# Attention and routed experts on one core: the sign turns of later groups and their adding transfers stand 4 to 11 half-steps later

## The chip, the cores and the metric

The kernel runs on one core of a Trainium2 chip. The metric is device time in microseconds (us) of one execution; the median of the runs is compared. Engine names in the rows are PE (TensorE matmul; PEld is its weight load), DVE (VectorE), ACT (ScalarE), POOL (GpSimd) and SP (SyncE, which here only issues transfers). A "q" behind a name is the engine's sequencer.

## What is computed

Attention over 32 heads (batch 4, 8 heads, 768 positions, 64 dimensions) in which a query sees only the keys of its own bucket, followed by a layer of eight experts with 384 places each:

```python
q_bits = (np.einsum('bhsd,dk->bhsk', q, proj) > 0)      # 6 sign bits make a bucket, keys alike
mask = q_bucket[:, :, :, None] == k_bucket[:, :, None, :]
scores = np.where(mask, scale * np.matmul(q, k.transpose(0, 1, 3, 2)), -1000000000.0)
scores = scores - np.max(scores, axis=-1, keepdims=True)
attn = np.exp(scores); attn = attn / (np.sum(attn, axis=-1, keepdims=True) + 1e-09)
x = np.matmul(attn, v)                                  # then rows of 512 = 8 heads x 64
# each row goes to one expert, best logits first: out = relu(x @ w1[e]) @ w2[e]
```

## The kernel before

Queries, keys and values are float32, and every product is made of float16 pairs: a rounded value ("high") and what rounding left over ("low"). The 32 heads are eight groups of four (G = 0 to 7). Of group G the transposed queries and keys are loaded to `qp` and `kp`. ACT rounds them to `qh` and `kh` (`cast`, line 147). The low parts `ql` and `kl` are `qp - qh` and `kp - kh`. In groups 1 and 2 POOL subtracts them (line 149). From group 3 on it is done in two other steps: ACT writes `-qh` into `ql` (`turn`, line 151, once for each of two head pairs), and then a transfer, issued by POOL, adds the float32 queries from memory onto it as it writes (`adds`, line 153). The same goes for the keys.

SP then moves high and low parts to where the matmuls read them: `qa`, `ka` get the high parts and sign bits, `qb` and `kb` a high and a low part. These are the moves (`moves`, with `go` at line 198, sign bits at line 204, clearing at line 214, next loads at line 76). `qa`, `ka`, `qb` and `kb` exist twice, for even and odd groups. The buffers `qp`, `kp`, `qh`, `kh`, `ql` and `kl` exist once: `turn` of one group writes the `ql` that the moves `qb<-ql` of the group before still have to read.

The main loop runs over 192 steps: six blocks of 128 keys for each head. In a step PE makes the score matmuls of a later head for its maxima (`S_pass`, line 265, reduced by DVE at line 267), the transposed scores of this head in two halves (`ST`, lines 314 and 315, into one of three buffers `pst`), and the product of weights and values four steps behind (`AV`, lines 337 to 339). ACT takes the exponential of each half (line 316, `pt<-pst`), and POOL or DVE makes its low part (`lo`, lines 320 and 323). The norm and the output of two heads follow (`XS`, low part on DVE at line 365, transfers by SP at line 375).

Other work is written into the loop by a table of half-steps: two in a step, 48 in a group. Entries count from the start of the group before, so half-step +1 of group G falls after the first scores of group G-1. For groups 4 to 7 the moves stand at +1 (high parts, sign bits, next `qp`) and +9 (clearing, next `kp`, then `kb<-kl` and `qb<-ql`). The table `Z4` places the turns at -31, -19, -25 and -13 (queries and keys of the first pair of heads, then of the second) and the adds at -19 (queries) and -11 (keys). As a group has 48 half-steps, -31 is +17 of the group before: eight half-steps behind the moves that read the same `ql`.

```python
def turn(G,w,p):
    A.activation(TMP[G,'l'][w][:,p],TMP[G,'h'][w][:,p],AF.Copy,scale=-1.0)
def adds(G,w):
    G_.dma_start(TMP[G,'l'][w]...,(qT,kT)[w][G]...,accum_op=ALU.add)
# in the loop over groups G, n = 0..3: w = n%2 (queries, keys), head pair n//2
z=AP['Z3'] if G==3 else [48*(G-1)+x for x in AP['Z4']]
add(z[n],turn,G,n%2,n//2)
if n<2: add(z[4+n],adds,G,n)
```

Every engine runs its instructions in the order in which they are written, and waits at the first that isn't ready.

Of the kernel before, what the change touches and what calls it, by code (L numbers as in the profile page):

```python
# [39 lines left out]
 LT=[362, 4],  # L40
 MS=74,
 Z3=[77,85,88,91,93,97],
 Z4=[-31,-19,-25,-13,-19,-11],
 EA=[262, 32, 5],
 EG={2: 0, 3: 3},
 MO=['', 'AKs', 'BqL', 'lmk', 'c|ABqKLslmk', 'ABqKLs|cklm', 'ABqKLs|cklm'],
# [9 lines left out]
def attention(tc, nc, ctx, qT, kT, vv, proj, wg, x_dram, L, jp, identf, ident, B, late=None, after=None):  # L56
# [343 lines left out]
    def add(n,f,*a):  # L400
        if n>=2*(6*NH+LAG+6): raise ValueError('an operation has no step')
        at.setdefault(n,[]).append((f,a))
# [15 lines left out]
    for G in range(1,NG):  # L418
# [5 lines left out]
        for n in range(4):  # L424
            if G<3: add(p[8+n],sub,G,n%2,n//2)
            else:
                z=AP['Z3'] if G==3 else [48*(G-1)+x for x in AP['Z4']]
                add(z[n],turn,G,n%2,n//2)
# [618 lines left out]
```

## Time and profile before

| | us |
|---|---|
| median of 3 runs (lowest, highest) | 743.61 (742.87, 745.62) |
| the profiled execution | 746.34 |
| its span | 744.6 |
| PE busy | 663.9 (89%) |
| DVE busy | 532.0 (71%) |
| POOL busy | 503.5 (68%) |
| ACT busy | 391.7 (53%) |

The attention takes a little more than the first half of the span and the experts the rest. PE is the busiest engine, and in most of the 40 slices of the page it is busy 90% or more; the dips in its first half are what there is to look at. To read them, one takes first who waited for whom, then the rows of the waiting engines in order of time.

### The profile page before, as it was taken

The numbers are of one execution on the slowest core, as the hardware profiler recorded it, in microseconds if no ns is written. First come the engines' busy times: TensorE is split into PE (matmuls) and PEld (weight loads), VectorE is DVE, ScalarE is ACT, GpSimd is POOL, SyncE is SP. The second block draws the span as 40 slices with busy tenths as digits, with TensorE's granted clock in tenths as the row PEclk, the third lists the DMA queues.
The fourth block names the chain that finished last, engine by engine and source line by source line (L and its number), as shares of the span: only waits on it lengthen the run. The fifth ranks groups of instructions, "written<-read, shape, count | busy, mean of one in ns | idle before, by whom it ended". The sixth has DMA issues, their size and how long they took to land. (4 is left out here: it accounts for less than half of the span.)

```text
span 744.6 us, 19011 instructions
## 1 busy us (share of the span) xinstructions
PE 663.9 (89%) x7761; PEld 425.5 (57%) x7769; DVE 532.0 (71%) x1230; ACT 391.7 (53%) x801; POOL 503.5 (68%) x464
## 2 busy tenths in 40 slices
PE   8999999499599688699999769999999999999994
PEld 2666666367366456467777556555555555555552
DVE  6879889378388486488898784989878887843120
ACT  6876886466466545567556225343535353444430
POOL 7799987367477456477775054485877878787761
PEclk9999999799799899899999759999999999999998
DMA  8649768667576655676131243536271717072601
GB/s 213 194 108 199 180 177 165 129 104 166 121 140 176 122 95 122 130 135 137 38 47 45 65 135 137 174 124 223 89 270 42 270 42 279 34 283 70 256 28 43
DMA packets 64299, 102.54 MB, mean 138 GB/s; under 512 B 28960, under 2 KB 53588, under 8 KB 62164
## 3 DMA queue, kind: packets, MB, share of 16 engines
q1 hardware_dynamic: 55236, 51.10, 29.0%
q0 software_dynamic: 8224, 50.08, 22.4%
q8 instruction: 61, 1.00, 0.6%
q10 hardware_dynamic: 752, 0.15, 0.1%
q14 instruction: 26, 0.21, 0.1%
HBM read 67.39 MB, written 12.58 MB: 107 GB/s over the span
## 5 line engine op out<-in xcount | busy, mean ns | idle before, releaser
L320 POOL TENSOR_TENSOR lo<-pt 128x768 f16<-128x768 f32 x148 | 240.3, 1644 | 105.5 <-ACT pt L316 96.5
L267 DVE TENSOR_REDUCE m<-pss 128x1 f16<-128x770 f32 x192 | 181.4, 956 | 71.3 <-PE pss L265 70.3
L316 ACT ACTIVATE pt<-pst 128x384 f32<-128x384 f32 x384 | 172.5, 489 | 100.6 <-PE pst L315 94.0
L314 PE MATMUL pst<-qa,ka 128*128 128x384 f16 x384 | 128.3, 335 | 38.3 <-ACT pt L316 33.8
L337 PE MATMUL psv<-vh,pt 128*128 128x65 f16 x1152 | 128.1, 197 | 3.4 <-DVE X L355 3.4
L315 PE MATMUL pst<-qb,kb 128*128 128x384 f16 x384 | 128.5, 335 | 0.0
L339 PE MATMUL psv<-vh,lo 128*128 128x65 f16 x1152 | 127.6, 196 | 0.8 <-POOL lo L320 0.6
L338 PE MATMUL psv<-vl,pt 128*128 128x64 f16 x1152 | 127.9, 195 | 0.0
L337 PEld LDWEIGHTS <-pt 128*128 128x128 bf16 x1152 | 109.3, 100 | 20.8 <-DVE X L355 5.3
L338 PEld LDWEIGHTS <-pt 128*128 128x128 bf16 x1152 | 108.2, 100 | 12.0 <-issue 1.7
L339 PEld LDWEIGHTS <-lo 128*128 128x128 f16 x1152 | 108.1, 99 | 1.2 <-POOL lo L320 0.9
L864 ACT CAST wh<-wf 128x1024 f16<-128x1024 f32 x64 | 65.4, 1042 | 76.7 <-DMA wf<-in_w_dram,zwidx 55.8
L265 PE MATMUL pss<-ka,qa 128*128 128x385 f16 x384 | 97.7, 339 | 7.2 <-DVE m L267 6.4
L876 POOL TENSOR_TENSOR wl<-wf,wh 128x512 bf16<-128x512 f32 x74 | 84.1, 1151 | 0.2 <-issue 0.2
L315 PEld LDWEIGHTS <-kb 128*128 128x128 f16 x384 | 38.1, 99 | 59.7 <-issue 39.5
L899 PEld LDWEIGHTS <-wh 128*128 128x128 f16 x544 | 50.6, 99 | 31.2 <-issue 1.4
L855 POOL DMA_INDIRECT wf<-in_w_dram,zwidx x20 | 19.9, 994 | 57.2 <-DVE zmi L788 30.6
L899 PE MATMUL ph<-xx,wh 128*128 128x384 f16 (+1 forms) x304 | 57.2, 313 | 0.4 <-issue 0.3
L911 PEld LDWEIGHTS <-hh 128*128 128x128 f16 x384 | 35.5, 97 | 36.3
L314 PEld LDWEIGHTS <-ka 128*128 128x128 f16 x384 | 38.3, 100 | 28.8 <-DMA qa<-mr 4.0
L899 PE MATMUL po<-xx,wh 128*128 128x384 f16 x240 | 48.1, 326 | 0.0
L986 POOL TENSOR_TENSOR wl<-wf,wh 128x512 bf16<-128x512 f32 x36 | 42.6, 1211 | 4.2 <-ACT wh L864 3.5
(292 smaller groups left out, 1215.8 us busy)
## 6 DMA issues: line engine op xcount, KB each, us to landing
vp<-in_vv_dram SPq DMA_DIRECT2D x8, 768.0 KB
x_dram<-XS SPq DMA_DIRECT2D x16, 384.0 KB
qp<-in_qT_dram SPq DMA_DIRECT2D x7, 768.0 KB
kp<-in_kT_dram SPq DMA_DIRECT2D x7, 768.0 KB
qa<-qh SPq DMA_DIRECT2D x14, 192.0 KB
ka<-kh SPq DMA_DIRECT2D x14, 192.0 KB
qb<-qh SPq DMA_DIRECT2D x14, 192.0 KB
kb<-kh SPq DMA_DIRECT2D x14, 192.0 KB
```

Source lines behind the costliest of these rows:

```text
L265: T.matmul(ps[:,hf,0:HK],QA[u][:,j,qc*128:qc*128+128],KA[u][:,j,hf*HK:hf*HK+HK],start=True,stop=True)
L267: V.tensor_reduce(M6[h][:,qc:qc+1],ps[:,:,0:HK],axis=AX.XY,op=ALU.max,negate=True)
L314: T.matmul(ps[:,0:384],KA[u][:,j,kr],QA[u][:,j,r],start=True,stop=False)
L315: T.matmul(ps[:,0:384],KB[u][:,j,kr],QB[u][:,j,r],start=False,stop=True)
L316: A.activation(PT[h,kc][0][:,r],ps[:,0:384],AF.Exp,scale=0.125)
L320: eng.tensor_tensor(l,p,p.bitcast(BF)[:,1::2],op=ALU.subtract)
L337: T.matmul(av[:,c,:],ph[:,r],VH[u][:,j,kc,:],start=(kc==0 and c==0),stop=False,skip_group_check=True)
L338: T.matmul(av[:,c,0:64],ph[:,r],VL[u][:,j,kc,:],start=False,stop=False,skip_group_check=True)
L339: T.matmul(av[:,c,:],l[:,r],VH[u][:,j,kc,:],start=False,stop=False,skip_group_check=True)
L864: s.nc.scalar.copy(h[:,r],f[:,r])
L876: for _ in range(n): s.nc.gpsimd.tensor_tensor(*s.pend.pop(0)[1],op=ALU.subtract)
L899: T.matmul(p[:,r],a[:,o:o+128],b[:,d,r],start=n==0 and not c,stop=n==11 and c in (None,2),skip_group_check=c is not None)
```

## The change

The table `Z4` gets other numbers. It serves groups 4 to 7; group 3 has a table of its own and groups 1 and 2 have no turns.

```diff
- Z4=[-31,-19,-25,-13,-19,-11],
+ Z4=[-20,-12,-18,-9,-15,-6],
```

So the query turns move from -31 and -25 to -20 and -18, the key turns from -19 and -13 to -12 and -9, and the adds from -19 to -15 (queries) and from -11 to -6 (keys). No instruction is added or taken away. PE's and SP's instructions stand in the same order in both, and so do DVE's.

ACT, between the value casts of group 4 and the keys of group 5 (`vh` is a value cast, `qh` and `kh` are the roundings, `ql` the turn, `pt` an exponential), before:

```order
L216 CAST vh_215<-vp 128x6x64
L151 ACTIVATE ql<-qh 128x768
L316 ACTIVATE pt<-pst 128x384
L216 CAST vh_215<-vp 128x6x64
L316 ACTIVATE pt<-pst 128x384
L147 CAST qh<-qp 128x384
L316 ACTIVATE pt<-pst 128x384 x2
L147 CAST qh<-qp 128x384
L316 ACTIVATE pt<-pst 128x384 x2
L151 ACTIVATE ql<-qh 128x768
```

The same engine in the changed kernel, from nine exponentials behind the place where the first turn stood (`mr` is a row of maxima, `shi` a sum of values):

```order
L282 ACTIVATE mr<-pst,mb_198,ms_199 24x128
L316 ACTIVATE pt<-pst 128x384
L231 CAST shi<-pst 32x256
L147 CAST kh<-kp 128x384
L285 DMA qa_171<-mr 4x6x128
L316 ACTIVATE pt<-pst 128x384
L151 ACTIVATE ql<-qh 128x768
L316 ACTIVATE pt<-pst 128x384 x2
L151 ACTIVATE ql<-qh 128x768
L316 ACTIVATE pt<-pst 128x384
L147 CAST kh<-kp 128x384
```

The first turn of the queries stood between two value casts; now eleven exponentials, both remaining roundings of the queries and two of the keys stand ahead of it. The key turns follow on the same engine:

```order
L316 ACTIVATE pt<-pst 128x384 x2
L363 CAST XS<-X 128x6x128
L316 ACTIVATE pt<-pst 128x384
L151 ACTIVATE kl<-kh 128x768
L316 ACTIVATE pt<-pst 128x384 x2
L282 ACTIVATE mr<-pst,mb_198,ms_199 24x128
L316 ACTIVATE pt<-pst 128x384
L151 ACTIVATE kl<-kh 128x768
```

The first key turn passed both later roundings of the keys, both turns passed the rounding of `XS`, and the second, which passed the row of maxima too, stands three exponentials behind the first instead of six.

On POOL, at the adds of group 5 (`lo` is a low part; `wt`, `wtb`, `tiny` are small constants), the changed kernel against the one before:

```order
-L153 DMA ql<-in_qT_dram 128x1536
 L574 TENSOR_SCALAR wt<-wt_88 128x8
+L153 DMA ql<-in_qT_dram 128x1536
 L575 TENSOR_SCALAR wtb<-wt_88 128x8
 L320 TENSOR_TENSOR lo<-pt 128x768 x2
-L153 DMA kl<-in_kT_dram 128x1536
 L551 MEMSET tiny 128x1
-L320 TENSOR_TENSOR lo<-pt 128x768 x8
+L320 TENSOR_TENSOR lo<-pt 128x768 x2
+L153 DMA kl<-in_kT_dram 128x1536
+L320 TENSOR_TENSOR lo<-pt 128x768 x6
```

The add of the queries passes one small constant and no low part, and the add of the keys passes two low parts.

## Rows read from the trace of the kernel before

**Rows 1.** Who waited for whom, whole run: us in total, times, longest.

```profile
PE pst L314 <- ACT pt L316: 33.8, 5, 9.9
ACT ql L151 <- DMA qb<-ql: 32.7, 4, 9.2
```

**Rows 2.** Timeline of ACT, the four waiting turns: start, length, instruction, [idle before <-releaser].

```profile
139.38 0.84 ACT L151 ACTIVATE ql<-qh 128x768 f16<-128x768 f16 x1 [9.20 <-DMA qb<-ql]
...
194.48 0.84 ACT L151 ACTIVATE ql<-qh 128x768 f16<-128x768 f16 x1 [8.91 <-DMA qb<-ql]
...
246.91 0.84 ACT L151 ACTIVATE ql<-qh 128x768 f16<-128x768 f16 x1 [7.86 <-DMA qb<-ql]
...
306.74 0.84 ACT L151 ACTIVATE ql<-qh 128x768 f16<-128x768 f16 x1 [6.75 <-DMA qb<-ql]
```

**Rows 3.** Timeline of SP, the end of the moves ahead of the second wait.

```profile
184.16 0.48 SPq L76 DMA_DIRECT2D kp<-in_kT_dram  x1
184.75 1.35 SPq L198 DMA_DIRECT2D kb<-kl  x2
186.20 1.39 SPq L198 DMA_DIRECT2D qb<-ql  x2
```

**Rows 4.** Timeline of PE at the second wait.

```profile
186.44 0.33 PE L315 MATMUL pst<-qb,kb 128*128 128x384 f16 x1
195.75 0.48 PE L314 MATMUL pst<-qa,ka 128*128 128x384 f16 x1 [8.99 <-ACT pt L316]
```

**Rows 5.** Stretches: window, us, busy of PE, PEld, DVE, ACT, POOL, granted clock, DMA share, GB/s.

```profile
139.50:145.00 5.50, 4.35 (x42) 2.99 (x42) 1.89 (x2) 4.56 (x11) 2.96 (x4) 0.50 0.34 95
195.00:200.30 5.30, 4.55 (x45) 3.18 (x45) 2.08 (x3) 4.36 (x11) 3.21 (x4) 0.50 0.26 78
...
247.00:252.00 5.00, 3.82 (x37) 2.46 (x37) 1.35 (x2) 4.25 (x11) 2.89 (x2) 0.53 0.40 109
268.00:278.00 10.00, 6.75 (x76) 3.61 (x74) 9.83 (x9) 1.98 (x6) 5.29 (x6) 0.88 0.73 121
278.00:300.00 22.00, 19.79 (x296) 14.38 (x295) 14.05 (x19) 13.36 (x32) 14.06 (x14) 0.90 0.58 132
307.00:312.00 5.00, 3.99 (x35) 2.63 (x35) 1.52 (x2) 4.06 (x10) 2.93 (x3) 0.50 0.36 101
```

**Rows 6.** Timelines of DVE, POOL and PE around 267 to 293 us.

```profile
267.43 5.97 DVE L365 TENSOR_TENSOR XS<-X,XS 128x768 f16<-128x768 f32 x1
...
267.32 0.86 POOL L153 DMA_DIRECT2D kl<-in_kT_dram  x1
...
274.32 0.49 PE L265 MATMUL pss<-ka,qa 128*128 128x385 f16 x2 [3.25 <-DVE m L267]
...
292.83 0.50 PE L314 MATMUL pst<-qa,ka 128*128 128x384 f16 x1 [2.21 <-DMA qa<-mr]
```

**Rows 7.** Line 365 over the whole run: count, shortest/median/longest in ns.

```profile
L365 DVE TENSOR_TENSOR XS<-X,XS x15: 944/1047/5966, 58.8 to 407.2; 128x768 f16<-128x768 f32 x15
```

**Rows 8.** Timeline of ACT behind the second wait.

```profile
206.07 0.87 ACT L316 ACTIVATE pt<-pst 128x384 f32<-128x384 f32 x2 [0.36 <-PE pst L315]
...
209.02 0.51 ACT L147 CAST kh<-kp 128x384 f16<-128x384 f32 x1
...
212.25 0.83 ACT L363 CAST XS<-X 128x768 f16<-128x768 f32 x1
```

**Rows 9.** Stretches before and in the second wait, columns as in Rows 5.

```profile
181.00:185.00 4.00, 4.00 (x76) 3.07 (x73) 4.00 (x4) 4.00 (x12) 4.00 (x4) 1.00 0.16 33
185.00:195.00 10.00, 1.76 (x24) 1.07 (x20) 4.04 (x7) 1.08 (x3) 2.59 (x3) 0.76 1.06 198
```

**Rows 10.** Adds: timeline of POOL, and time from issue to landing of line 153.

```profile
160.58 0.86 POOL L153 DMA_DIRECT2D kl<-in_kT_dram  x1
...
210.39 3.95 POOL L320 TENSOR_TENSOR lo<-pt 128x768 f16<-128x768 f32 x2 [3.50 <-ACT pt L316]
...
DMA to landing us min/median/max: 6.1/6.2/9.6
```

## The prediction

> **What bounds the kernel now.** The page says that PE is busiest, so I read first what PE waits for. The list of waits has one entry that is few and long: five waits for a score buffer that ACT had to empty, 33.8 us in all and up to 9.9 us each [rows 1]. ACT itself was held just then: four waits of the turn for the transfer `qb<-ql`, 32.7 us [rows 1]. The timeline of ACT shows them one by one, 9.20, 8.91, 7.86 and 6.75 us, one for each of groups 4 to 7 [rows 2]. This is a write after a read: the turn may overwrite `ql` only when the last move of the group before has read it.
>
> The second of them serves as the pattern. ACT arrives at 194.48 - 8.91 = 185.57 us [rows 2]. SP issues `qb<-ql` at 186.20 us, so even later than ACT arrives, behind the load of `kp` and the moves `kb<-kl` [rows 3], and the data have been read only at 194.48. All exponentials stand behind the turn on ACT; PE starts its last score matmul at 186.44 and the next at 195.75 us, 8.99 us idle [rows 4]. Then it pays a second time: in the 5.30 us from 195.00 the granted clock is 0.50, the level of 1.2 GHz, and the other three waits are followed by 5.50, 5.00 and 5.00 us at 0.50, 0.53 and 0.50 [rows 5].
>
> **What the stalls are worth.** The four PE stalls are nearly all of the 33.8 us [rows 1]; I take 33.6. Half a clock costs half of such a stretch: 2.75 + 2.65 + 2.35 + 2.50 = 10.25 us [rows 5].
>
> A third sum comes from comparing the groups. ACT's arrivals at the turn are at 130.18, 185.57, 239.05 and 299.99 us (start less wait, [rows 2]). The distances are 55.4, 53.5 and 60.9 us. Less the stall within each (the ACT waits serve: 9.2, 8.9, 7.9) and the slow clock behind it (2.75, 2.65, 2.35), 43.4, 41.9 and 50.7 us are left. The last is longer than the second by 8.8 us. Its cause stands at 267.43 us: the low part of an output takes DVE 5.97 us [rows 6] where the median is 1.05 [rows 7]. It began 0.11 us after POOL began to issue the add of the keys [rows 6]. PE waits 3.25 us for DVE, later 2.21 us for a row of maxima [rows 6], and loses 0.12 x 10 + 0.10 x 22 = 3.4 us to the clock [rows 5]: 8.9 us, the same sum by another way. I call this the incident.
>
> **The change part by part.** Nothing is added: the same eight query and eight key turns of 0.84 us and eight adds run at other places. What counts is whether each finds its data ready and whom it holds up.
>
> First the query turn. Eleven exponentials now stand ahead of it. In the trace the eleventh of these begins at 206.07 and takes half of 0.87 us [rows 8], so it ends at 206.5. From PE's restart at 195.75 that is 10.75 us, of which 4.55 at half clock; at full clock 8.5. PE would go on at 186.6 instead (its last start, 186.44, and half of 0.33, since matmuls overlap), so ACT reaches the turn at 186.6 + 8.5 = 195.1 us. The read ends at 194.48 [rows 2]. The margin is 0.6 us. For the others I add the same 9.5 us to the old arrival and subtract the old wait: 0.3, 0.6, 1.6 and 2.7 us. So all four waits go, but two only just. A landing later by x costs x less this margin.
>
> What is late next is the rounding of the keys, which waits for `kp`. It now comes after eight exponentials, some 5 us after the old arrival, at 190.6 us. `kp` is issued at 184.16 [rows 3]; 768 KB at the 198 GB/s of that stretch [rows 9] take 4.0 us, so an estimate from these two, with the 0.48 us of the issue, is 188.6. [...] Cost 0 to 3.9 us; I take 0, since the estimate leaves 2.0 us.
>
> The turns now stand closer. From the eleventh exponential to the twenty-second ACT has 12 x 0.435 (exponentials), 4 x 0.84 (turns), 2 x 0.51 (roundings) [rows 8], 0.83 for the output [rows 8] and under 0.51 for the maxima: 10.9 us. The group rate of 41.9 us in 48 half-steps gives 12 half-steps 10.5 us. ACT falls behind by 0.4 us there, by somewhat more at the worst point, and PE has three score buffers to cover it. Cost 0 to 1.5 us a group; I take 0.7, nearer to 0.4. It cannot gain.
>
> The adds: POOL waits for the later query turn, but stands idle there anyway, 3.50 us before its next low part [rows 10], since DVE makes two low parts. The add of the keys starts two low parts later, 210.39 to 214.3 being such a pair [rows 10], so about 3 to 4 us: in place of 160.58 [rows 10] at 164.5. At the longest landing, 9.6 us [rows 10], it has landed by 175, and the first move that reads it is issued at 184.75 [rows 3]. Cost 0, with 10 us of cover; SP, and behind it the outputs and the next loads, would pay if that were used up. DVE's order is unchanged.
>
> Against this stands a page of the Trainium skill, "DMA: Bandwidth & Descriptors", section "Issuing engines are not separate DMA queues": transfers issued by different engines share the same 16 DMA engines. The add of the keys moves towards the moves, and by this rule would make them later. The trace agrees that they share something: in the wait itself the DMA share is 1.06 [rows 9]. Before it, though, from 181 to 185 us, it is 0.16 [rows 9], so that what is pushed back at the start has 3.4 us of free engines ahead of `kp`. An add of 384 KB is 1.9 us at 198 GB/s.
>
> The sum: 33.6 + 10.25 + 8.9 = 52.7 us to be had; less 4 x 0.7 = 2.8 for ACT and 0.2 for the narrow margins, 49.7 us. From the median 743.61 that is **694 us**; against the profiled execution's own 746.34 (span 744.6) it would be 696.6, the 2.7 us between the two being the profiled run's own. The expert stage follows unchanged, only earlier.
>
> **The rivals.** *The incident stays.* It may have nothing to do with the add: each group has two such DVE instructions, and POOL makes low parts most of the time. For its going: the add of the keys no longer stands beside that instruction, and only one of 15 took over 5 us [rows 7]. Price 8.9 us: 703 us. The Trainium skill, "SBUF — State Buffer", section "Who interferes with whom", says that a DVE instruction with two inputs there and a GpSimd one exclude each other for the whole instruction, whoever starts first. By that rule the incident belongs to any low part and stays; the 5.97 us are more than one low part on POOL, so the rule alone doesn't explain them.
>
> *A wait remains* at the query turn or, before it, at the rounding of the keys: the burst grows by the 1.9 us of the add, or `kp` is late by up to 3.9. With 3 us a group and, after 2 to 3 us of idle PE, some 1.5 us of clock (the incident's 3.25 and 2.21 us of idleness cost 3.4 together, [rows 5, 6]), 4 x 4.5 = 18 us: 712 us. With half of that, 703. For it: a margin of 0.3 us. Against: the gap in the DMA share.
>
> *Slower.* The add of the keys lands after `kb<-kl` wants to go. SP then waits, with `qb<-ql` and the outputs behind it, and the next query turn waits on. It begins to cost when the landing takes over 20 us (164.5 to 184.75), and the kernel is slower than before when it takes over 31, as the saved 11 us a group are then spent; at 35 us the four groups lose 16 net: 760 us. Against: the longest of the landings shown is 9.6 us [rows 10].
>
> *No effect:* the wait changes only its name, since `kp` or the output of SP's queue ends at the same 194.48 whatever stands there. But eleven exponentials no longer stand behind it, so this takes a new cause: 743 us.
>
> **How the numbers follow.** Waits and incident gone, 694 us (690 to 698): 0.50. Incident, or one like it, stays, 703: 0.24. A wait remains, 699 to 712: 0.16. More than the sum, below 690: 0.05. No effect 0.02, slower 0.03. The range leaves out the last three and the upper end of the remaining wait: 688 to 710. A measurement of this kernel tells about 0.5%, 3.7 us, from no change, so faster 0.95, same 0.02, slower 0.03.
>
> **What would show it.** Right: no entry `ql <- DMA qb<-ql` above 1 us in the waits; PE without a stall above 2 us between 125 and 300 us; clock 1.00 where it was 0.50; first query turns about 42 us apart; line 365 below 2.5 us. Wrong: line 147 on `kh` or line 151 on `ql` waiting 2 us or more, SP waiting for an add, or POOL's add waiting while `lo` is due. The prediction falls if the read of `ql` ends later against PE's steps than it does now.

## The result, and the profile after

The changed kernel takes 703.49 us (median) against 744.62 us of the kernel before beside it: ratio 0.945, 95% interval 0.940 to 0.950, a gain of 41.1 us. The time lies in the predicted range, 9.5 us above the predicted value. A later measurement of both gave 703.88 against 743.41 us, 0.9463 (0.9418 to 0.9508). The rows of after are those of the execution profiled there (701.03 us, span 699.2), because the one profiled first was disturbed.

First the list of waits, for PE, ACT and POOL, from 105 to 340 us (releaser behind the arrow; us in total, times, longest):

```profile
PE psv L337 <- DVE X L355: 7.0, 7, 1.8
PE pst L314 <- DMA qa<-mr: 1.6, 2, 1.3
PE pst L314 <- ACT pt L316: 1.6, 5, 0.5
PE pst L280 <- DVE m L275: 1.3, 4, 0.5
...
ACT kh L147 <- DMA kp<-in_kT_dram: 0.9, 1, 0.9
...
POOL ql L153 <- ACT ql L151: 11.3, 4, 3.1
```

The first line of [rows 1], 33.8 us, is down to 1.6 us, and its second, the turn's wait for `qb<-ql`, has no entry any more. What is now first on PE, the wait for the norm, stood fourth in the same list of before, behind the 33.8 us and these two:

```profile
PE pst L314 <- DMA qa<-mr: 3.3, 2, 2.2
PE pss L265 <- DVE m L267: 3.3, 1, 3.3
PE psv L337 <- DVE X L355: 2.9, 3, 1.1
```

The turns, on ACT's timeline, start without a wait, where [rows 2] had 9.20, 8.91, 7.86 and 6.75 us:

```profile
139.35 0.84 ACT L151 ACTIVATE ql<-qh 128x768 f16<-128x768 f16 x1
...
184.19 0.84 ACT L151 ACTIVATE ql<-qh 128x768 f16<-128x768 f16 x1
...
227.91 0.84 ACT L151 ACTIVATE ql<-qh 128x768 f16<-128x768 f16 x1
...
272.85 0.83 ACT L151 ACTIVATE ql<-qh 128x768 f16<-128x768 f16 x1
```

The second of them again serves as the pattern. SP issues the moves that read `ql` of the group before at 174.44 us, so 9.75 us before the turn; in [rows 2, 3] they went out 0.63 us after ACT had arrived at it:

```profile
172.34 0.53 SPq L76 DMA_DIRECT2D kp<-in_kT_dram  x1
172.99 1.35 SPq L198 DMA_DIRECT2D kb<-kl  x2
174.44 1.46 SPq L198 DMA_DIRECT2D qb<-ql  x2
```

To see where the time went, I cut both traces at the same four places of the program, one group (48 half-steps) each. Before (columns as in Rows 5: window, us, busy of PE, PEld, DVE, ACT, POOL, granted clock, DMA share, GB/s):

```profile
112.80:170.60 57.80, 45.43 (x684) 32.35 (x683) 39.32 (x55) 32.49 (x74) 34.45 (x32) 0.91 0.69 139
170.60:224.00 53.40, 43.21 (x633) 30.79 (x632) 37.21 (x50) 32.10 (x75) 34.55 (x30) 0.90 0.67 137
224.00:281.10 57.10, 45.63 (x683) 32.42 (x681) 41.21 (x50) 32.73 (x78) 34.20 (x28) 0.91 0.61 128
281.10:336.40 55.30, 45.14 (x634) 31.57 (x633) 35.76 (x49) 31.77 (x72) 33.24 (x29) 0.91 0.64 132
```

After:

```profile
112.10:159.10 47.00, 43.04 (x685) 30.90 (x683) 42.18 (x55) 32.28 (x74) 36.27 (x32) 1.00 0.82 168
159.10:202.80 43.70, 41.16 (x633) 29.33 (x632) 38.48 (x50) 31.96 (x75) 36.16 (x30) 1.00 0.83 168
202.80:247.40 44.60, 42.37 (x683) 30.60 (x681) 39.65 (x50) 32.51 (x78) 36.18 (x28) 1.00 0.78 160
247.40:291.40 44.00, 41.50 (x634) 29.26 (x633) 37.68 (x49) 31.31 (x72) 35.27 (x29) 1.00 0.84 171
```

The four groups shrink from 223.6 to 179.3 us, by 44.3 of the 45.3 us between the two profiled executions. PE's instructions are the same and take 179.4 and 168.1 us: 11.3 us come back because the granted clock is 1.00, the level of 2.4 GHz, throughout. PE's idle time falls from 44.2 to 11.2 us, by 33.0. The medians differ by less, 41.1 us (40.7 with the 703.88 us measured where the profile was taken), since the profiled execution of before was 1.7 us above the median of 744.62 and that of after 2.9 us below its own.

### The profile page after: what moved, and what is told of

It reads as the page before. It is cut to its first block, busy times and chain, and to the rows that moved or that the text cites. A ratio compares the mean times of both kernels' runs of the same rounds, so it can differ in the third digit from the quotient of the medians.

```text
span 712.3 us, 19019 instructions
## 1 busy us (share of the span) xinstructions
PE 654.6 (92%) x7761; PEld 421.5 (59%) x7769; DVE 535.4 (75%) x1230; ACT 391.0 (55%) x801; POOL 510.9 (72%) x464
## 5 line engine op out<-in xcount | busy, mean ns | idle before, releaser
L320 POOL TENSOR_TENSOR lo<-pt 128x768 f16<-128x768 f32 x148 | 246.5, 1681 | 48.4 <-ACT pt L316 44.4
L314 PE MATMUL pst<-qa,ka 128*128 128x384 f16 x384 | 126.0, 328 | 8.2 <-DMA qa<-mr 4.0
L337 PE MATMUL psv<-vh,pt 128*128 128x65 f16 x1152 | 124.9, 195 | 6.9 <-DVE X L355 6.9
L315 PE MATMUL pst<-qb,kb 128*128 128x384 f16 x384 | 126.1, 329 | 0.0
L339 PE MATMUL psv<-vh,lo 128*128 128x65 f16 x1152 | 124.9, 194 | 0.1
L338 PE MATMUL psv<-vl,pt 128*128 128x64 f16 x1152 | 124.9, 193 | 0.0
L337 PEld LDWEIGHTS <-pt 128*128 128x128 bf16 x1152 | 107.6, 98 | 24.1 <-DVE X L355 9.5
L338 PEld LDWEIGHTS <-pt 128*128 128x128 bf16 x1152 | 106.5, 99 | 11.0 <-issue 0.3
L339 PEld LDWEIGHTS <-lo 128*128 128x128 f16 x1152 | 106.5, 98 | 0.3 <-DVE lo L320 0.3
L265 PE MATMUL pss<-ka,qa 128*128 128x385 f16 x384 | 95.1, 332 | 7.3 <-DVE m L267 2.9
```

What stands on the lines that cost most here:

```text
L265: T.matmul(ps[:,hf,0:HK],QA[u][:,j,qc*128:qc*128+128],KA[u][:,j,hf*HK:hf*HK+HK],start=True,stop=True)
L314: T.matmul(ps[:,0:384],KA[u][:,j,kr],QA[u][:,j,r],start=True,stop=False)
L315: T.matmul(ps[:,0:384],KB[u][:,j,kr],QB[u][:,j,r],start=False,stop=True)
L320: eng.tensor_tensor(l,p,p.bitcast(BF)[:,1::2],op=ALU.subtract)
L337: T.matmul(av[:,c,:],ph[:,r],VH[u][:,j,kc,:],start=(kc==0 and c==0),stop=False,skip_group_check=True)
L338: T.matmul(av[:,c,0:64],ph[:,r],VL[u][:,j,kc,:],start=False,stop=False,skip_group_check=True)
```

## The experiments

Two theories were to be told apart at first. The one predicted: ACT's turn has to wait for the read of the single buffer `ql`. Its rivals: something else in the new order makes the gain, the closer adds for one, or the wait only hides a load that is late anyway.

### The same kernel once more

No edit.

> The changed kernel once more, for a profile that stands beside its median. Theory (the turn's wait for the read of ql was the cost): 701 to 705 us; no turn waits for qb<-ql; what is missing to the 694 us forecast shows as small waits of PE, each under 2 us, in the groups with turns. Rival (the incident of 5.97 us on DVE stays): one DVE instruction of line 365 over 4 us and PE idle over 3 us at one place.

706.44 us against 741.78, ratio 0.953 (0.9495 to 0.9564): 1.4 us above the range that was expected. The gain is somewhat less than in the two other measurements of this kernel (0.945 and 0.946); the intervals overlap. The rest came as the theory said: no turn waits for `qb<-ql`, line 365 takes 2.22 us at most, and PE's longest wait from 105 to 340 us is 1.8 us.

### A second buffer for the low queries, nothing moved

```diff
-TMP[G,'l']=[dp.tile([128,2,S],F16,name=n,bufs=1) for n in ("ql","kl")]
+TMP[G,'l']=[dp.tile([128,2,S],F16,name=n,bufs=2-i) for i,n in enumerate(("ql","kl"))]
```

The table is that of before, so no instruction stands at another place; the turn just writes another buffer than the one being read.

> The kernel before with its old table, and a second buffer for ql, so that the turn overwrites nothing that a move still reads. Every instruction stands where it stood. Theory (a write after a read was the whole cost): 694 to 706 us, without the wait of the turn, and PE's stalls of 7 to 10 us gone. Rival (the later place itself helps, through the transfers): 715 us or more.

704.31 us, ratio 0.9506 (0.9468 to 0.9543): the whole gain, without a move (the changed kernel beside it took 706.44 us). The turn's wait and the four stalls are gone from its waits, while one row of before has stayed:

```profile
PE psv L337 <- DVE X L355: 3.4, 5, 1.1
PE pst L314 <- DMA qa<-mr: 3.3, 2, 2.1
PE pss L265 <- DVE m L267: 3.2, 1, 3.2
```

So what the change removes is the write after a read, as predicted. The third line is the incident, which this kernel keeps.

### Only the queries' steps; only the keys' steps; only the keys' add

```diff
- Z4=[-31,-19,-25,-13,-19,-11],
+ Z4=[-20,-19,-18,-13,-15,-11],   # queries
+ Z4=[-31,-12,-25,-9,-19,-6],     # keys
+ Z4=[-31,-19,-25,-13,-19,-6],    # the keys' add alone
```

> Only the queries' part of the change: query turns at -20 and -18 and their add at -15, key turns and their add where they were (-19, -13, -11). Theory (only the query turn waited): 698 to 705 us, as the whole change, perhaps 1 to 3 us less than it, since ACT's turns are spread wider. Rival (the keys' part brings a share, through the transfers or the incident): 708 us or more.

> The other half of the change alone: key turns at -12 and -9, their add at -6, the queries' turns and add where they were. Theory: the four waits for qb<-ql stay, and the time is that of the kernel before, 741 to 746 us; line 365 without 5.97 us, line 173 near 1.9 us. Rival (the keys' part carries some of the 40 us): below 738 us.

> The kernel before with one entry of its table changed: the add of the keys at -6 in place of -11. All turns stay, and with them the four waits for qb<-ql. Theory (the 5.97 us of line 365 in group 6 come from the add that stands beside it): the incident goes, which is worth 8.9 us, of which the next group's wait takes back about 2, as it grows from 6.8 to near 9: 735 to 740 us where before has 742 to 744. Rival (the incident belongs to any low part that POOL makes): line 365 still takes over 5 us somewhere, 741 to 745 us.

Queries alone: 705.52 us, 0.9513 (0.948 to 0.9547), as good as the whole change beside it (706.44 us), though half a microsecond above the range expected. Keys alone: 746.13 us, 1.0029 (0.9993 to 1.0065). The keys' add alone: 744.23 us, 1.0005 (0.9974 to 1.0035), where a gain of some us from the vanished incident was expected; that missed. In both kernels without the queries' move the turn waits as before; the waits of keys alone and, second, of the add alone:

```profile
ACT ql L151 <- DMA qb<-ql: 33.0, 4, 9.4
...
ACT ql L151 <- DMA qb<-ql: 32.9, 4, 8.7
...
PE psv L337 <- DVE X L355: 6.7, 4, 1.9
```

The incident did go with the keys' add, as line 365 shows. Here it is in the kernel with two buffers, then in the one with the add alone, then in the whole change (count, then shortest/median/longest in ns):

```profile
L365 DVE TENSOR_TENSOR XS<-X,XS x15: 946/1270/5966, 58.3 to 364.4; 128x768 f16<-128x768 f32 x15
...
L365 DVE TENSOR_TENSOR XS<-X,XS x15: 945/1593/2270, 58.2 to 403.2; 128x768 f16<-128x768 f32 x15
...
L365 DVE TENSOR_TENSOR XS<-X,XS x15: 943/1347/2221, 58.1 to 362.2; 128x768 f16<-128x768 f32 x15
```

The long one takes 5.97 us in every kernel that has the add at -11 (before, two buffers, queries alone, half the way, there a second one of 5.76 us), and at most 2.27 us in all that have it at -6. But in its place the norm's wait has grown from 2.9 to 6.7 us.

### Half the way

```diff
- Z4=[-31,-19,-25,-13,-19,-11],
+ Z4=[-25,-19,-23,-13,-19,-11],
```

> The query turns moved half the way: -25 and -23, their add and the keys where they were. Six half-steps are about 5.2 us (41.9 us in 48), so of the waits 9.2, 8.9, 7.9 and 6.8 the theory leaves 4.0, 3.7, 2.7 and 1.6: 12 us above the whole change, and up to 6 more where the clock still falls: 713 to 722 us. Rival (the first half of the way is enough): within 3 us of the whole change.

730.47 us, 0.9833 (0.9788 to 0.9877): 11 us gained, at least 8 us short of the 713 to 722 us expected. Its waits, then a stretch of 5.5 us behind the first of them:

```profile
ACT ql L151 <- DMA qb<-ql: 17.7, 4, 4.9
...
PE pst L280 <- ACT pt L316: 14.9, 4, 4.5
...
139.00:144.50 5.50, 3.75 (x21) 2.42 (x21) 0.00 (x0) 3.38 (x9) 3.59 (x5) 0.62 0.38 109
```

Six half-steps took 15 of the 32.7 us off the turns' waits, 3.75 us each; the prediction's 9.5 us for eleven would make it 5.2 each. Why each half-step brings less here was not settled. A second line 365, of 5.76 us, also costs PE 3.2 us that the kernel before doesn't have. And the clock falls behind the shorter stalls too, in the stretch shown to a mean of 0.62. The mean granted clock of the execution, 0.951 before, 0.960 here and 0.976 in the whole change, looks as if a third of it had come back. But the work in the four groups, between the same two places of the program as above, shows none of it:

```profile
112.30:323.60 211.30, 180.29 (x2628) 126.74 (x2627) 159.53 (x204) 128.10 (x299) 141.41 (x116) 0.94 0.70 142
```

PE is busy for 180.3 us here, 179.4 before and 168.1 in the whole change. All that was gained in these groups is idle time, 13.2 us (44.2 to 31.0).

### The incident's worth, and whether the keys' place matters

```diff
+ bufs=2-i as above, and Z4=[-31,-19,-25,-13,-19,-6],   # two buffers, add at -6
+ Z4=[-20,-19,-18,-13,-15,-6],                          # queries, add at -6
```

> Two buffers for ql with the old turns, and the add of the keys at -6. Theory: neither the waits for qb<-ql nor the incident; 3 to 7 us below the two buffers alone, 697 to 701 us. Against it works that the multiplication of the sign bits (line 173) then meets low parts and takes near 1.9 us in place of 1.0, which the theory prices at 0.6 us of PE a group: 2.4 us given back. Rival (the incident moves elsewhere): within 2 us of two buffers alone.

> Query turns and both adds as in the change (-20, -18; -15, -6), only the key turns where they were (-19, -13). It differs from the whole change in the key turns alone. Theory (what the keys' part costs comes from the add and line 173, not from ACT's crowded turns): within 2 us of the whole change, line 173 near 1.9 us. Rival (ACT's crowding costs 0.7 us a group): 2 to 4 us below the whole change.

703.78 us, 0.9447 (0.9401 to 0.9493), and 704.43 us, 0.9462 (0.942 to 0.9504). The second shows no difference from the key turns' place: it is the whole change without them, and within 1 us of two of that kernel's three measurements (703.49 and 703.88 us, the third is 706.44; none of them was taken beside it). The first missed its expectation: taking the incident away from the kernel with two buffers brought 0.5 us by the medians (704.31 and 703.78 us, not taken side by side), not several. The group of the incident, with two buffers, then with the add at -6 too:

```profile
201.60:249.70 48.10, 43.99 (x683) 31.68 (x681) 40.64 (x50) 32.07 (x78) 35.02 (x27) 0.96 0.71 152
...
204.00:248.60 44.60, 42.46 (x681) 30.61 (x682) 39.80 (x51) 32.11 (x78) 36.01 (x28) 1.00 0.79 164
```

That group is 3.5 us shorter, 1.5 of it PE's busy time at the better clock; a wait of 1.6 us for the norm, which lies in it only in the latter kernel, is already taken off. In the list of that kernel the norm's wait, 3.4 us with two buffers alone, gives most of the gain back:

```profile
PE psv L337 <- DVE X L355: 7.5, 7, 1.9
```

### Why the norm is late, and a kernel that does without it

The place is the base of each group. DVE makes the sign bits there (line 173) ahead of the norm (lines 351 to 355). After, DVE, then POOL, then PE:

```profile
196.72 1.89 DVE L173 TENSOR_SCALAR bt<-bt 128x768 f16<-128x768 f16 x1
198.53 0.95 DVE L267 TENSOR_REDUCE m<-pss 128x1 f16<-128x770 f32 x1
...
199.81 0.56 DVE L355 TENSOR_TENSOR X<-psv,r 128x384 f32<-128x384 f32 x1
...
196.00 0.88 POOL L153 DMA_DIRECT2D kl<-in_kT_dram  x1
196.63 1.76 POOL L320 TENSOR_TENSOR lo<-pt 128x768 f16<-128x768 f32 x1
...
200.43 0.20 PE L337 MATMUL psv<-vh,pt 128*128 128x65 f16 x1 [1.42 <-DVE X L355]
```

The add at its new place puts POOL's low part, 196.63 to 198.39, beside line 173, which ends 0.2 us after it. Before, the add stood earlier and only the end of a low part met line 173. Its instructions of the four groups, from 112 to 340 us, before and after (shortest/median/longest in ns):

```profile
L173 DVE TENSOR_SCALAR bt<-bt x4: 360/1302/1390, 164.7 to 330.9; 128x768 f16<-128x768 f16 x4
...
L173 DVE TENSOR_SCALAR bt<-bt x4: 1753/1924/1970, 152.6 to 285.4; 128x768 f16<-128x768 f16 x4
```

By the Trainium skill, "SBUF — State Buffer", section "Who interferes with whom", an instruction of this kind may use the port pair that DVE shares with GpSimd, and then whoever has the pair keeps it for a whole instruction. The trace agrees: 0.36 us alone (before, in the group of the incident, where POOL had finished), 1.89 us beside a low part of 1.76.

To test it, ACT multiplies the sign bits of groups 4 to 7 as well, as it does in groups 2 and 3:

```diff
-        if G in (2,3): A.activation(bt,bt,AF.Copy,scale=8192.0)
+        if G>1: A.activation(bt,bt,AF.Copy,scale=8192.0)
```

> The whole change, and in groups 4 to 7 the sign bits are multiplied by ACT (line 172, as groups 2 and 3 do) in place of DVE (line 173). Theory (line 173 held up by POOL makes the norm late, and PE waits 1.3 to 1.8 us for it in each of four groups): these waits fall under 0.7 us, 3 to 5 us below the whole change. Rival (the norm is late for another reason, or ACT's 0.84 us holds PE as much): no gain, 702 to 706 us.

> The whole change beside the two kernels below on one chip: 702 to 706 us.

> The whole change with the sign bits multiplied by ACT, again: theory, 2 to 4 us below the whole change, since PE no longer waits for a late norm. Rival (the 3 us of the first look were the run's): within 1 us.

> Two buffers for ql, turns at their old places, keys' add at -6, sign bits multiplied by ACT. Theory: no long wait, no incident, no late norm, and ACT's turns spread out: 0 to 3 us below the whole change with ACT's multiplication, 698 to 702 us. Rival (the turns' places do not matter once nothing waits): within 1 us of it.

On the whole change: 701.53 us, 0.9425 (0.9375 to 0.9475), and repeated with the whole change beside it on the same chip 699.79 us, 0.9416 (0.9358 to 0.9474), against 703.88 us. With two buffers and the old turns: 701.84 us, 0.9444 (0.939 to 0.9497). The first has the lowest medians of all, both times. Against the whole change it is 4.1 us, where 2 to 4 were expected, but its six times (697.0 to 707.2) overlap those of the whole change (701.0 to 705.2), so the gain itself is not shown. The kernel with two buffers lies 2.0 us above it and not below, by six times (698.9 to 706.8) that overlap as well: turns that are spread out bring nothing that shows. The mechanism is shown: the norm's wait is all but gone. Others have taken its place, from the same list:

```profile
PE pst L314 <- DMA qa<-mr: 4.7, 3, 2.2
PE pst L229 <- ACT pt L316: 4.0, 5, 1.9
...
PE psv L337 <- DVE X L355: 0.6, 2, 0.3
```

Its four groups take 179.0 us in the profiled execution, where those of the whole change take 179.3. Where the lower medians come from is therefore left open.

## Why the prediction was right, and where its sum was off

**The four stalls: right.** Forecast 33.6 us; PE's wait for ACT at line 314 fell by 32.2 us (33.8 to 1.6). Two buffers without a move give the same gain and the keys' steps alone give none, so the cause is the read of `ql`, shown from both sides. The measured time alone wouldn't have told: 703.49 us is what two of the rivals had priced, 703 us for an incident that stays and 703 for half of a remaining wait, and both are refuted by the rows, not by the time.

**The clock: right in kind, too large.** The prediction took 10.25 us for the stretches at half clock and 3.4 us for those behind the incident, 13.65 in all; 11.3 came back. The step that failed is "half a clock costs half of such a stretch". The stretches begin before PE does: their idle part, 1.15, 0.75, 1.18 and 1.01 us [rows 5], is the end of the stall, which the 33.6 us already hold. In the same way the two stretches behind the incident hold its 3.25 and 2.21 us of waiting [rows 5, 6]. The clock's price is on what PE works: 0.50 x (4.35 + 4.55 + 3.99) + 0.47 x 3.82 is 8.2 us, and 0.12 x 6.75 + 0.10 x 19.79 is 2.8 us [rows 5], together 11.0 us, near to the 11.3 by which PE's busy time fell.

**The incident: its place right, its worth too large.** It goes with the keys' add, against the rival that kept it. But of its three parts only the 3.25 us went altogether; the waits for `qa<-mr`, 3.3 us in all, fell to 1.6. Measured between kernels without the four stalls it is 3.5 us in its group, 2.0 of idle PE (net of 1.6 for the norm) and 1.5 of clock, and net almost nothing, since the moved add brings the norm's wait with it. The second way to 8.9 us, by comparing groups, agreed partly by chance: the group it measured against is the shortest of the three (634 matmuls of PE against 682 in the group of the incident), and the same two groups still differ by 1.2 us after the change, without an incident.

**What costs something: the wrong item.** The prediction charged 2.8 us for turns that crowd on ACT. With the key turns left where they were the time is the same (704.43 us), and so it is with two buffers and all four turns at their old, wider places (703.78 us with the add at -6): there is no sign of that cost. PE's wait for ACT at line 314 is 1.6 us in all. The cost came at a place the prediction had called unchanged, DVE, through POOL: the norm's wait grew by 3.8 us (2.9 before, 6.7 from 112 to 291 us after), and line 280's wait for `m` by 1.3 us. The prediction asked of the moved add who waits for its data, and not what POOL does beside DVE right after it.

Together, by terms of idle PE: forecast 39.1 less 3.0, measured 33.0 us; with 11.3 us of clock 44.3 in place of 49.7 us. Outside the four groups the two profiled executions differ by another 1.0 us, and the way back from their 45.3 us to the 41.1 of the medians is the place of the two in their own spread.

**Margins and adds.** No turn waits, so even the margin of 0.3 us held or was larger. `kp` is waited for once, 0.9 us; the prediction took 0 and left up to 3.9 us a group. No run shows that upper bound. What the runs show is that the estimate behind the 0 was too short: `kp` landed 5.8 us after its issue here (129.45 to 135.23 us) and 9.0 in the kernel with the queries' steps alone (215.05 to 224.06, where ACT waited 2.6 us), not 4.5. POOL waits 11.3 us for the turns in front of its adds, and PE's list has no wait for a low part behind them; this comes near one of the prediction's signs of being wrong, without a cost to PE. The rule on shared DMA engines that the prediction weighed was not put to the test. The DMA share of a group rose from 0.61 to 0.69 up to 0.78 to 0.84, but those are the same transfers in less time (0.69 x 57.8 = 39.9 us of work in the first group before, 0.82 x 47.0 = 38.5 after). The adds land later, where [rows 10] had a median of 6.2 us:

```profile
DMA to landing us min/median/max: 6.0/7.2/9.9
```

Nothing that PE waits for shows it, and the moves still end before the turn.

**The signs.** No wait of `ql` for `qb`, no PE stall over 1.8 us between 125 and 300 us, clock 1.00, line 365 at 2.22 us: four as forecast. The first query turns were to be about 42 us apart; they are 44.8, 43.7 and 44.9. It was this sign that showed the missing 2 to 3 us a group.

## What to carry to other kernels

When an engine with queued work behind it stands at a write, look for the transfer that still reads the old contents: a later write or a second buffer is worth the whole stall of everyone behind, and the clock that PE loses after it. Price the clock by PE's busy time in the slow stretch, not by a stretch that holds the end of the stall, and don't expect it back in proportion: with stalls half as long PE's busy time had not fallen at all. When a transfer issued by POOL is moved, look at which DVE instruction the next POOL instruction will now run beside.

## What was not expected of the hardware

A DVE instruction with two inputs in SBUF was held through three low parts of POOL in a row, at the same place in each of the four kernels with the add at -11, where it began 0.11 us after POOL began to issue the add. DVE, then POOL, of the kernel with two buffers:

```profile
236.32 5.97 DVE L365 TENSOR_TENSOR XS<-X,XS 128x768 f16<-128x768 f32 x1
...
236.21 0.86 POOL L153 DMA_DIRECT2D kl<-in_kT_dram  x1
236.82 3.17 POOL L320 TENSOR_TENSOR lo<-pt 128x768 f16<-128x768 f32 x2
...
239.73 1.73 POOL L320 TENSOR_TENSOR lo<-pt 128x768 f16<-128x768 f32 x1
```

It ends at 242.29 us, 0.8 us behind the last of them. The 5.76 us of the half-way kernel began 0.26 us after POOL began to issue the add. But the start by itself doesn't decide it. In the same four kernels the line 365 of an earlier group also began 0.11 us after its add, and took 0.95 us; in the kernel before (the add stands at 160.58 in [rows 10]):

```profile
160.69 0.95 DVE L365 TENSOR_TENSOR XS<-X,XS 128x768 f16<-128x768 f32 x1
...
161.17 0.39 POOL L551 MEMSET us<- 128x1 bf16 x1
161.23 4.58 POOL L320 TENSOR_TENSOR lo<-pt 128x768 f16<-128x768 f32 x3
```

There a small memset stands on POOL between the add and the low parts. Whether that is what let DVE through is not shown. So the prediction's cause of the incident, the add beside it, is only part of it: with the add moved away no line 365 is that long, but in an earlier group the same nearness cost nothing.

Elsewhere the meeting of the two lengthens line 365 to 2.27 us at most, so by no more than one low part of 1.73. The section of the Trainium skill named above lets one instruction go first, which fits the 2.27; why DVE lost three times here is open and was not tried.
